# Where the load of S2 stands in the order of issue

## The chip, the cores and the metric

The kernel runs on one core of one Trainium2 chip. The metric is the device time of one execution in microseconds. The engines of the core run instruction queues of their own: TensorE (PE in the profile) multiplies matrices, its weight loads are shown as PEld; VectorE (DVE), ScalarE (ACT) and GpSimd (POOL) do elementwise work; SyncE (SP) issues DMAs. ScalarE can issue DMAs too. An engine's instructions run in the order in which they stand in its queue, and wait on semaphores that other engines or landed DMAs raise.

## The reference

An attention with a polynomial sketch as its feature map, followed by a Fourier mixing layer with an MLP. Cut to what matters here:

```python
# batch 4, heads 4, seq 1088, head_dim 32, r 8; S1, S2: [8, 32]
def phi(x):
    a = np.einsum('rd,bhsd->bhsr', S1, x)
    b = np.einsum('rd,bhsd->bhsr', S2, x)
    return np.einsum('bhsi,bhsj->bhsij', a, b).reshape(*x.shape[:-1], r * r)
q_p, k_p = phi(q), phi(k)
kv = np.einsum('bhsf,bhsd->bhfd', k_p, v)
z = np.sum(k_p, axis=2)
x = np.einsum('bhsf,bhfd->bhsd', q_p, kv) / (np.einsum('bhsf,bhf->bhs', q_p, z)[..., None] + 1e-06)
# x as [batch, seq, 128]
u = x + np.real(fft(fft(x, axis=1), axis=2))
out = u + np.maximum(normalised(u) @ w_ch1, 0) @ w_ch2
```

Everything in the attention goes through S1 and S2: both are needed, transposed, before the first feature of q or k can be computed.

## The kernel before

The program is a list of named steps, each with an engine. Nothing schedules them: a hand-written string, `ORDER`, gives the order of issue of all steps, and so the order within each engine's queue. A second table (`BANK`) gives each step its banks of PSUM, and `BEHIND` lets a SyncE load wait for an earlier one, counted back in SyncE's list of transfers.

The steps that matter for the change:

- `ld_s1` (SyncE) and `ld_s2` (ScalarE), both line 108, load S1 into rows 0 to 7 and S2 into rows 8 to 15 of one small tile, `s12`, in four copies side by side (4 KB each, in pieces of 128 bytes).
- `a_sin` (ScalarE, line 251) is an activation whose only purpose is to load ScalarE's first table.
- `warm` and `FILL` (TensorE, lines 90 and 92) are matmuls on zeros whose results nobody reads. Four stand at the start, others are put before a step: one in fp32 and two in bf16 before `s_t`, three in bf16 before `qf0.0` and `qf0.1`.
- `c_idb` (GpSimd) builds an identity, `c_id16` (ScalarE, line 308) casts its corner.
- `s_t` (TensorE, line 341) transposes `s12` with that corner. It waits for both loads and for `c_id16`.
- `s_use` (VectorE, lines 346 to 349) makes three tiles of the result: `sblk` for the projections of k, `sa` and `sb` for the features of q.
- `qT` (VectorE, line 430) and `kT` (line 381) transpose q and k; `qf` (TensorE, line 437) and `kpr` (line 363) project them; `qa` and `kab` (ScalarE, lines 444 and 415) copy one factor out of PSUM, `qp` (VectorE, line 448) and `kp` (GpSimd or VectorE, line 104) multiply the two factors.
- `vc` (ScalarE or GpSimd, line 97) rearranges v, `kv` (TensorE, line 397) and `pnd` (line 483) are the two products of the attention, and `den`, `rden`, `x` (lines 490, 495, 498) divide.

The four batches follow one another through these steps, overlapping; then come the Fourier rows (line 523) and the mixer by tiles of 512 rows. All loads but `ld_s2` are issued by SyncE: two halves of q of batch 0, S1, two halves of k of batch 0, two halves of q of batch 1, then v, the remainders of q and k (`qt`, `kt`), and the later batches. Buffers are double or triple, so loads of later batches wait for readers of the earlier ones.

Each DMA signals on one of eight semaphores, given out in rotation; a DMA that takes a semaphore again first waits until the previous DMA on it has landed. In the program of before, `ld_s2` stands on the same semaphore as `ld_s1`. It stands behind `a_sin` in ScalarE's queue.

Of the kernel before, what the change touches and what calls it, by code (L numbers as in the profile page):

```python
# [877 lines left out]
}  # L878

ORDER = """  # L880
c_wz warm ld_q0.0 c_iota c_rows ld_q0.1 ld_s1 c_bias c_eo1 a_sin ld_s2 c_xd0 ld_k0.1 c_vt0 c_more c_vt1 c_kk t_turn1
t_turn3 c_idb t_ph3 ld_k0.0 ld_q1.0 ld_q1.1 ld_v0.0 qT0.0 c_id16 s_t t_ph1 c_cen c_mask qT0.1 s_use ld_qt c_v10 kT0.1
ld_v0.3 ld_kt kT0.0 qf0.0 ld_k1 ld_v0.2 kpr0.1 ld_v0.1 ld_vt0 c_v11 ld_vt1 d_turn qa0.0 t_turn2 l_turn ld_v1.0 qT1.0
kpr0.0 ld_q2.1 t_ph2 kab0 qp0.0 qT1.1 qf0.1 c_kvz t_cos1 t_sin1 c_sgn kp0.3 ld_v1.3 kp0.1 qa0.1 ld_v1.2 qf1.0 qa1.0
# [51 lines left out]
```

## Time and profile before

| | |
|---|---|
| median of 3 runs | 89.14 us (89.13 to 90.52) |
| the profiled execution | 89.34 us |
| its span, first to last instruction | 87.3 us |
| mean granted TensorE clock | 0.961 |
| busy: TensorE matmuls, VectorE, ScalarE, GpSimd | 73.7, 63.8, 52.2, 49.6 us |
| DMA queue of SyncE | 15896 packets, 10.13 MB |
| DMA queue of ScalarE | 184 packets, 0.14 MB |

The span is that of the profile; what lies between it and the 89.34 us is start and end of the execution. Busy times of the engines overlap, and a high share only says that an engine works most of the time. What sets the time is read from the chain of work that ended last, which follows back from the last instruction, at each step, to what released it. The transfers are listed in it as DMA with the tile they fill; the tile `s12` appears as `t_s`.

### The profile page before, as it was taken

What the parts mean: (1) busy time and instruction counts of PE and PEld (TensorE: products, weight loads), DVE (VectorE), ACT (ScalarE), POOL (GpSimd) and SP (SyncE); (2) the same over time, 40 slices, a digit from 0 to 9 for tenths busy, and PEclk for the clock granted to TensorE, in tenths of its full rate; (3) what the DMA queues carried; (4) which work ended last, traced back from release to release, by engine and by line L of the source; (5) the groups of instructions that cost most, each with busy time, mean ns of one, the idle gap of its engine ahead of it and who ended that gap; (6) DMA issues with size and microseconds to landing.
All of it is one profiled execution on the core that took longest, in us unless ns stands there. A gap on an engine that the chain in (4) does not pass through costs nothing.

```text
span 87.3 us, 3321 instructions
## 1 busy us (share of the span) xinstructions
PE 73.7 (84%) x1380; PEld 53.4 (61%) x1380; DVE 63.8 (73%) x185; ACT 52.2 (60%) x94; POOL 49.6 (57%) x78
## 2 busy tenths in 40 slices
PE   5950399978997999989999779999999998898920
PEld 1300247436896868869794577797677575574920
DVE  5770292949999495799199985968796788877940
ACT  6020004763788855768718459274998698988620
POOL 7888300599739999879999970040599362100000
PEclk9999555899999999999999999999999999999999
DMA  0999599456984827910000020901202496423072
GB/s 15 266 265 261 106 249 234 76 151 187 304 265 135 275 62 220 245 30 0 8 8 8 0 60 0 66 2 21 46 0 60 135 67 181 156 105 138 25 261 103
DMA packets 16095, 10.47 MB, mean 120 GB/s; under 512 B 6864, under 2 KB 14544, under 8 KB 16080
## 3 DMA queue, kind: packets, MB, share of 16 engines
q1 hardware_dynamic: 15896, 10.13, 45.9%
q8 instruction: 10, 0.16, 0.9%
q10 hardware_dynamic: 184, 0.14, 0.5%
q14 instruction: 5, 0.04, 0.2%
HBM read 7.22 MB, written 2.23 MB: 108 GB/s over the span
## 4 chain that ended last, share of the span: by engine, by line
PE 46%; ACT 16%; DVE 14%; DMA 14%; issue 3%; POOL 1%; SPq 1%; DVEq 0%; ACTq 0%
DMA t_s<-in_S_dram 9%; PE ps L483 8%; PE ps L437 7%; PE ps L649 6%; PE ps L665 6%; PE ps L397 5%; DMA t_unT__166<-t_un__161 4%; PE ps L363 4%; ACT t_ht__168 L656 4%; PE ps L92 3%; DVE t_qp__124 L448 3%; DVE t_zr__139 L547 2%; ACT t_qa__123 L444 2%; PE ps L523 2%; PE ps L460 2%
## 5 line engine op out<-in xcount | busy, mean ns | idle before, releaser
L104 POOL TENSOR_TENSOR t_kp__118<-t_ab__116 128x512 f32<-128x512 f32 x7 | 7.3, 1068 | 7.7 <-ACT t_ab__116 L415 7.7
L444 ACT COPY t_qa__122<-ps 128x1024 f32<-128x1024 f32 x4 | 4.0, 1012 | 9.2 <-PE ps L437 9.2
L92 PE MATMUL ps<-t_wz 128*128 128x512 bf16 x18 | 7.5, 512 | 1.9 <-DVE t_wz L173 1.0
L104 POOL TENSOR_TENSOR t_kp__119<-t_ab__117 128x512 f32<-128x512 f32 x7 | 7.4, 1085 | 1.9 <-ACT t_ab__117 L415 1.9
L656 ACT ACTIVATE t_ht__168<-ps 128x1024 bf16<-128x1024 f32 x6 | 6.0, 1022 | 0.7 <-PE ps L649 0.7
L656 ACT ACTIVATE t_ht__167<-ps 128x1024 bf16<-128x1024 f32 x5 | 5.1, 1022 | 1.5 <-DVE t_st__147 L596 0.8
L483 PE MATMUL ps<-t_kvz,t_qp__124 128*64 128x66 f32 x128 | 4.3, 224 | 1.6 <-DVE t_qp__125 L448 1.1
L444 ACT COPY t_qa__123<-ps 128x1024 f32<-128x1024 f32 x4 | 4.0, 1012 | 2.6 <-PE ps L437 2.6
L483 PEld LDWEIGHTS ps<-t_kvz,t_qp__124 128*64 128x64 f32 x128 | 4.0, 137 | 1.9 <-DVE t_qp__125 L448 1.2
L649 PEld LDWEIGHTS <-t_w1b 128*128 128x128 bf16 x40 | 3.2, 97 | 3.0 <-issue 2.1
L448 DVE TENSOR_TENSOR t_qp__124<-ps,t_qa__122 128x1024 f32<-128x1024 f32 x2 | 2.4, 1224 | 3.3 <-ACT t_qa__122 L444 3.3
L397 PEld LDWEIGHTS ps<-t_v__121,t_kp__119 128*64 128x64 f32 x128 | 4.1, 138 | 0.7 <-issue 0.7
L92 PEld LDWEIGHTS <-t_wz 128*128 128x128 bf16 x18 | 1.7, 115 | 4.4 <-issue 3.1
L483 PEld LDWEIGHTS ps<-t_kvz,t_qp__125 128*64 128x64 f32 x128 | 3.9, 137 | 0.8 <-ACT t_kvz L97 0.4
L397 PE MATMUL ps<-t_v__121,t_kp__119 128*64 128x33 f32 x128 | 4.4, 224 | 0.0
L397 PE MATMUL ps<-t_v__120,t_kp__118 128*64 128x33 f32 x128 | 4.3, 223 | 0.0
L104 POOL TENSOR_TENSOR t_eo__133<-t_xd__132 128x516 bf16<-128x516 bf16 x4 | 4.1, 1050 | 0.2
L483 PE MATMUL ps<-t_kvz,t_qp__125 128*64 128x66 f32 x128 | 4.2, 223 | 0.0
L448 DVE TENSOR_TENSOR t_qp__124<-ps,t_qa__123 128x1024 f32<-128x1024 f32 x2 | 2.4, 1224 | 2.4 <-ACT t_qa__123 L444 2.4
L397 PEld LDWEIGHTS ps<-t_v__120,t_kp__118 128*64 128x64 f32 x128 | 4.1, 138 | 0.1
L341 PE MATMUL ps<-t_id,t_s 16*128 16x16 f32 x1 | 0.3, 253 | 4.6 <-DMA t_s<-in_S_dram 4.6
L97 ACT COPY t_kvz<-ps 64x66 f32<-64x66 f32 x8 | 1.7, 209 | 3.9 <-PE ps L397 3.4
(272 smaller groups left out, 233.2 us busy)
## 6 DMA issues: line engine op xcount, KB each, us to landing
t_q_in__109<-in_q_dram SPq DMA_DIRECT2D x4, 256.0 KB, 3.2
t_v_in__107<-in_v_dram SPq DMA_DIRECT2D x8, 128.0 KB, 4.2
t_k_in__106<-in_k_dram SPq DMA_DIRECT2D x2, 512.0 KB
t_v_in__108<-in_v_dram SPq DMA_DIRECT2D x8, 128.0 KB, 4.3
t_k_in__105<-in_k_dram SPq DMA_DIRECT2D x2, 256.0 KB
t_q_in__110<-in_q_dram SPq DMA_DIRECT2D x2, 256.0 KB
t_q_in__111<-in_q_dram SPq DMA_DIRECT2D x2, 256.0 KB
t_k_in__105<-in_k_dram SPq DMA_DIRECT2D x1, 512.0 KB
```

Source lines behind the costliest of these rows:

```text
L92: nc.tensor.matmul(T("ps")[:, free, :], w[:, 0:128], bass.AP(tensor=w.tensor, offset=w.offset, ap=[list(w.ap[0]), [0, 4], [1, 128]]), star ...
L104: return (nc.vector if engine == DVE else nc.gpsimd).tensor_tensor(out=out, in0=in0, in1=in1, op=op)
L363: nc.tensor.matmul(ps(use, 64 * t, [[1, 64]], 64 * c, 64), view(src, 128 * t + 64 * c, [[1, 64]]), T("sblk")[:], start=True, stop=True, ti ...
L397: nc.tensor.matmul(ps(f"kv{b}", 33 * pr, [[1, 33]], 64 * c, 64), kp, v, start=(t == 0), stop=(t == 8), tile_position=(0, 64 * c), skip_gro ...
L437: nc.tensor.matmul(ps(f"q{b}.{pr}", 512 * g + 256 * w, [[1, 256]], 64 * h, 64), view(T(src), 0, [[1, F]], 32 * g, 32), view(T(f"qT{b % 2}" ...
L444: nc.scalar.copy(T(f"qa{pr}")[:], ps(f"q{b}.{pr}", 0, [[512, 4], [1, 256]]))
L448: nc.vector.tensor_tensor(out=view(T(f"qp{b % 2}"), 1024 * pr, [[32, 4], [128, 8], [1, 32]]), in0=ps(f"q{b}.{pr}", 256, [[512, 4], [32, 8] ...
L460: nc.tensor.matmul(ps("qt", 512 * j + 256 * w + 128 * (h // 2), [[1, 128]], 64 * (h % 2), 64), view(T(src), 0, [[1, F]], 32 * j, 32), view ...
L483: nc.tensor.matmul(ps(f"nd{b}", 512 * (s // 3) + 132 * (s % 3) + 66 * pr, [[1, 66]], 64 * c, 64), w, view(T("kvz"), 132 * b + 66 * pr, [[1 ...
L649: nc.tensor.matmul(ps(use, 128 * n * i, [[1, 128 * n]]), T("w1b")[:, 128 * c:128 * c + 128], own("unT", g)[:, 0:128 * n], start=True, stop ...
L656: nc.scalar.activation(out=out, in_=in_, func=ACT.Relu)
L665: nc.tensor.matmul(ps(u, where, [[1, 128]]), view(own("ht", g), (128 if g % 5 == 4 else 512) * c + 128 * t, [[1, 128]]), T("w2b")[:, c, :] ...
```

## The change

One name moves in `ORDER`, from behind `a_sin` to the second place:

```diff
 ORDER = """
-c_wz warm ld_q0.0 c_iota c_rows ld_q0.1 ld_s1 c_bias c_eo1 a_sin ld_s2 c_xd0 ld_k0.1 c_vt0 c_more c_vt1 c_kk t_turn1
+c_wz ld_s2 warm ld_q0.0 c_iota c_rows ld_q0.1 ld_s1 c_bias c_eo1 a_sin c_xd0 ld_k0.1 c_vt0 c_more c_vt1 c_kk t_turn1
```

In the built program this has two effects. ScalarE's queue begins with the DMA instruction of `ld_s2`, then comes the table load, then `a_sin`; the queues of the other engines hold the same instructions in the same order. And since `ld_s2` is now the first DMA of the program, the rotation of the eight semaphores starts with it: `ld_s2` waits for nothing, and the loads of SyncE that follow stand one semaphore further. The waits that differ for this are those of the first eight or so loads that reuse a semaphore:

| load of SyncE | waits before for | waits after for |
|---|---|---|
| v, first part of batch 0 | S1 | S1 and S2 |
| q remainder, 4 parts | q half 0, q half 1, first k, second k | q half 0, q half 1, (nothing new), first k |
| v, last part of batch 0 | first q of batch 1 | second k |
| k remainder | second q of batch 1 | first q of batch 1 |
| k of batch 1 | v, first part of batch 0 | second q of batch 1 |

The arithmetic is the same.

## The prediction

> **What bounds the kernel now.** I read the page's slices first, then the chain of waits, then the timelines of ScalarE, TensorE and SyncE over the first microseconds.
>
> ```profile
> PE   5950399978997999989999779999999998898920
> PEclk9999555899999999999999999999999999999999
> DMA  0999599456984827910000020901202496423072
> ```
>
> Each digit is the busy share of 2.18 us. TensorE works in the first slices, has a hole in the fourth and fifth (about 6 to 10 us), and is then on a low clock for three slices; from there on it is nearly always busy. So the only large hole is at the start, and the chain of waits, in order of time, says what it waits for:
>
> ```profile
> 1.78 2.85 DMA t_s<-in_S_dram
> 4.63 0.02 issue
> 4.65 5.26 DMA t_s<-in_S_dram
> 9.91 0.14 issue
> 10.04 0.25 PE ps L341
> 10.30 1.39 PE ps L92 x3
> 11.69 1.94 PE ps L437 x32
> 13.63 1.91 PE ps L363 x32
> 15.53 0.88 PE ps L92 x3
> 16.42 1.13 PE ps L437 x32
> 17.55 0.02 issue
> ```
>
> Columns are start, length and what. The load of S1 lands at 4.63. The load of S2 is issued 0.02 us later and needs 5.26 us, and only then can the transpose of S1 and S2 (step s_t, L341) run, on which all projections (L437 of q, L363 of k) depend. Those then run at half clock: the same three fills take 1.39 us at 10.30 and 0.88 at 15.53, the same 32 matmuls of a q feature 1.94 us at 11.69 and 1.13 at 16.42.
>
> ```profile
> 0.71 1.28 ACT L251 ACT_TABLE_LOAD   x1 [0.71 <-PEq L920]
> 2.01 0.20 ACT L251 ACTIVATE t_scr<-t_hpi 128x1 f32<-128x1 f32 x1
> 4.65 0.58 ACTq L108 DMA_DIRECT2D t_s<-in_S_dram  x1
> 5.27 0.20 ACT L308 CAST t_id<-t_idb 16x16 f32<-16x16 bf16 x1 [3.06 <-POOL t_mask L101]
> ```
>
> ScalarE is free at 2.21 and issues S2 only at 4.65. In the program of before the load of S2 signals on the same one of the eight DMA semaphores as the load of S1, and so first waits for S1's landing. The table load and the activation cost it little; that wait costs it 2.44 us, and the position behind a full DMA queue the rest.
>
> **The change part by part.** S2's load becomes ScalarE's first instruction, at about 0.71. It becomes the first DMA, takes the first semaphore, and waits for nothing. No instruction is added or removed. The instructions of TensorE, VectorE, GpSimd and SyncE keep their order; the semaphores rotate by one, so some waits name another transfer.
>
> *ScalarE.* The issue takes 0.58 us (row at 4.65), so table load and activation end at about 2.8 instead of 2.21. The next ScalarE work, the identity's cast at 5.27, waited behind S2's issue; without it, it runs when GpSimd's identity is ready, before 5.27. Cost: nothing, under an idle stretch of 3.06 us.
>
> *SyncE.* Its loads are issued in the same order:
>
> ```profile
> 0.72 1.01 SPq L143 DMA_DIRECT2D t_q_in__109<-in_q_dram  x2
> 4.64 0.80 SPq L129 DMA_DIRECT2D t_v_in__107<-in_v_dram  x1
> 7.97 0.31 SPq L129 DMA_DIRECT2D t_v_in__107<-in_v_dram  x1
> 9.60 0.39 SPq L113 DMA_DIRECT2D t_kt_in<-in_k_dram  x1
> ```
>
> The load of v at 4.64, issued beside S2, took 0.80 us, a like one alone 0.31: two issues at once cost SyncE up to 0.49 us. Now q's first load, at 0.72, is the one beside S2, so every load behind it may slip by 0 to 0.49; I take 0.35. Against this, the rotation makes v at 7.97 wait for a load one earlier (k instead of q), the k remainder at 9.60 for the first q half of batch 1 instead of the second (which v at 7.97 waited for), and the 512 KB of k behind it for that second half. I put the two together at nothing for the loads after 10 us. The load of v at 4.64 now waits for S2 as well as S1; S2 is ahead of S1 by a microsecond at the issue, so that costs nothing unless S2 is starved (a rival below).
>
> *The transpose s_t.* Three things gate it. S1: 4.63, or 5.1 with the slip. S2: issued at 0.71; the two rows for a landing of this size are 2.85 (S1, nearly empty queues) and 5.26 us (S2, full ones), so 3.6 to 6.0; I take the shorter, since at 0.71 the queues are as empty as they were for S1. And TensorE's own queue, fills that run until 5.48:
>
> ```profile
> 1.04 1.89 PE L92 MATMUL ps<-t_wz 128*128 128x512 bf16 x4 [1.04 <-DVE t_wz L173]
> 4.42 1.06 PE L92 MATMUL ps<-t_wz 128*128 128x512 bf16 x2
> ```
>
> So s_t starts at 5.5 in place of 10.04: **4.54 us earlier** (4.0 if S2 takes 5.26 us). The fills are the cover for the slip of S1.
>
> The Trainium skill speaks against expecting more from the second issuer: "DMA: Bandwidth & Descriptors", section "Issuing engines are not separate DMA queues", says that transfers issued by different engines run on the same 16 DMA engines and interleave, and that only issue time is saved. By that alone S2 would share with the first q load, and the sum would be the same; the 0.80 and 0.58 us above show that here even the issue isn't free.
>
> *The clock.* Granted clock by stretch:
>
> ```profile
> core 0: us, PE busy (x) PEld busy (x) DVE busy (x) ACT busy (x) POOL busy (x), PEclk, DMA share, GB/s
> 0.00:5.50 5.50, 4.45 (x8) 1.39 (x8) 4.03 (x25) 1.72 (x4) 4.23 (x21) 1.00 0.56 163
> 5.50:8.90 3.40, 0.00 (x0) 0.00 (x0) 0.60 (x1) 0.28 (x1) 2.95 (x6) 1.00 1.07 262
> 8.90:15.70 6.80, 5.66 (x69) 3.25 (x70) 3.59 (x8) 1.13 (x2) 0.54 (x1) 0.50 0.92 196
> ```
>
> The full clock was granted from 5.5 to 8.9, where TensorE did nothing; after that idle stretch it fell to 0.50 until 15.7. With s_t at 5.5 there is no idle stretch, and I take it that the full clock stays. Three terms shrink to their full-clock twins: fills 1.39 to 0.88, q feature 1.94 to 1.13, k projection 1.91 to 1.15 (row below). Together **2.08 us**. The row's 1.00 before 5.5 isn't borne out by the durations: 1.89/4 = 0.47 us per fill is the half-clock value (1.39/3 = 0.46).
>
> The Trainium skill, "TensorE: Matmul & The Clock Gate", Part 1, says that half rate is the default, and that a free-running window of about 3.4 us decides, so its phase may differ between runs. The trace agrees on an idle stretch of that length (5.5 to 8.9) followed by 0.50; what another phase would do is the first rival.
>
> What VectorE does in between must keep up. Its last q transpose ends at 6.10, the three ops on S gave way to the next after 0.40 us (10.41 to 10.81), and the two k transposes took 1.29:
>
> ```profile
> 5.40 0.70 DVE L430 STREAM_TRANSPOSE t_qT__114<-t_q_in__109 128x512 f32<-128x512 f32 x1
> 10.41 0.22 DVE L346 TENSOR_TENSOR t_sblk<-ps,t_mask 128x64 f32<-128x64 f32 x1 [4.31 <-PE ps L341]
> 10.81 1.29 DVE L381 STREAM_TRANSPOSE t_kT__112<-t_k_in__105 128x512 f32<-128x512 f32 x2
> 23.07 1.15 PE L363 MATMUL ps<-t_sblk,t_kT__113 128*64 128x64 f32 x32
> ```
>
> So S is ready at about 6.5, just before the fills end (5.5 + 0.25 for s_t + 0.88 = 6.63), the q feature runs to 7.8, and the k transposes end at 7.9 if k has landed, just in time. The second q feature then ends at 17.55 - 4.54 - 2.08 = 10.93: 6.62 us earlier.
>
> *What is late next: the loads.* They do not start earlier, and the compute behind them comes 6.6 us sooner. The tightest ones:
>
> ```profile
> t_q_in__109<-in_q_dram SPq DMA_DIRECT2D x4, 256.0 KB, 3.2
> 19.93 0.43 SPq L143 DMA_DIRECT2D t_q_in__111<-in_q_dram  x1
> 27.81 0.69 DVE L430 STREAM_TRANSPOSE t_qT__114<-t_q_in__111 128x512 f32<-128x512 f32 x1
> 29.66 0.38 DVE L495 RECIPROCAL t_den__126<-t_den__126 128x36 f32<-128x36 f32 x1 [1.16 <-ACT t_den__126 L490]
> SPq L129 <- DMA t_k_in__105<-in_k_dram: 1.5, 1, 1.5
> 29.24 0.31 SPq L129 DMA_DIRECT2D t_v_in__107<-in_v_dram  x1
> 32.63 1.20 DVE L381 STREAM_TRANSPOSE t_kT__112<-t_k_in__105 128x1024 f32<-128x1024 f32 x1
> 34.85 1.22 DVE L448 TENSOR_TENSOR t_qp__124<-ps,t_qa__123 128x1024 f32<-128x1024 f32 x1 [1.01 <-ACT t_qa__123 L444]
> ```
>
> The second q half of batch 2, issued at 19.93, lands by the median of 3.2 us at 23.1. Its transpose would be wanted at 27.81 - 6.62 = 21.2: 1.9 us late, of which the 1.16 us that VectorE idles before the reciprocal absorbs most, so 0.75 is given back. The k of batch 2 lands at 29.24 (the v load waits for it) and would be wanted at 26.0: 3.2 late, of which 1.01 is idle before the next product: 2.2 given back. That landing may itself move, since SyncE's later waits on compute go away. I take the middle, **1.4 us given back**. Beyond 38 us no inputs are loaded, and the shift carries through to the end.
>
> Sum: 4.54 + 2.08 - 1.4 = 5.2 us. The profiled execution took 89.34 us (span 87.3 and 2.0 around it), which gives 84.1; the median is 0.2 below the profiled run: **83.9**. Its own range, from no give-back (6.6) to all of 2.2 (4.4): 82.5 to 84.8.
>
> **The rivals.** *Half clock at first* (0.13): the release comes only after 12.3, at the second boundary. The terms at half clock stay, the fills at 15.53 become half-clock ones (+0.51), and the shift is 4.54 - 0.51 = 4.0: 85.1. For it: TensorE's durations before 5.5 are half-clock ones. Against it: the row for 5.5 to 8.9 grants 1.00.
>
> *The loads decide all* (0.13): no idle time absorbs, and what can be won is the slack of k of batch 2, 32.63 - 29.24 = 3.4 us: 85.7. For it: the DMA slices are 9s from 2 to 9 us and again from 11 to 15. Against it: the idle times in the rows above.
>
> *No effect* (0.07): S2, in 128-byte pieces, still lands near 10 us, because its queue gets little service beside SyncE's until the DMA slices drop; the load chain's slip stays inside its slack: 89.
>
> *Slower* (0.07): the same late S2, but now the load of v at 4.64 waits for it, since it has S2's semaphore, and all loads behind it on SyncE with it. With S2 at 9.9 they slip by 5.3 us; k of batch 2 lands at 34.5, 1.9 us after its transpose began: 91.0. It decides from a slip of 3.4 us, that is from S2 landing after 8.0. For it: 5.26 us for 4 KB in before. Against both: S1, of the same size and behind 512 KB of q in its queue, took 2.85.
>
> **How the numbers follow.** The forecast has 0.60, with 83.9. The range must reach the first two rivals: 82.3 to 86.0 holds nearly all of the forecast, half clock and most of the load case, about 0.82. A difference of 2% is 1.8 us, about what the runs of before can tell from none (89.13 to 90.52). Faster: 0.60 + 0.13 + 0.13 = 0.86; within: 0.07; slower: 0.07.
>
> **What would show it.** S2's issue as ScalarE's first row; s_t directly behind the fills, at 5.5; no slice with an empty TensorE before 10 us and no 5s in its clock; the second q feature ending near 11; and new waits of VectorE or ScalarE on loads of q, v or k between 18 and 30 us, which the chain of waits should name. I am wrong if s_t still waits for a DMA beyond 6 us, if the v load of 4.64 is issued much later, or if the clock falls in spite of a busy TensorE.

## The result and the profile after

| | before | after |
|---|---|---|
| median | 89.21 us (89.13 to 90.52, 4 runs) | 82.78 us (82.31 to 84.42, 4 runs) |
| profiled execution, its span | 89.34, 87.3 us | 82.31, 80.2 us |

The ratio is 0.9264, with a 95% interval of 0.9202 to 0.9326: 6.4 us between the medians. The forecast was 83.9. Measured twice more on other chips, the same kernel gave 0.9394 (0.9265 to 0.9522; 83.98 against 88.51 us) and 0.9435 (0.9335 to 0.9535; 84.02 against 88.55 us). The medians of the three sets differ by 6.4, 4.5 and 4.5 us where 5.2 were forecast, so the gain is sure and its size is known to about a microsecond either way. What follows compares mainly kernels of one set, which share the runs of the kernel before. Some executions of every kernel run some per cent longer than the rest; the ratios leave these out on both sides, the medians do not.

The page's slices of the profile after, each 2.0 us:

```profile
PE   4999995998899998999995999989999979899910
PEclk9999999999999999999999999999999999999999
DMA  0989979648597970982002120020032955314082
```

The hole of TensorE between 6 and 10 us is gone, and with it the 5s in its clock. The timeline of the first microseconds (start, length, engine, line, what):

```profile
0.71 0.60 ACTq L108 DMA_DIRECT2D t_s<-in_S_dram  x1
0.72 1.01 SPq L143 DMA_DIRECT2D t_q_in__109<-in_q_dram  x2
...
4.70 0.68 SPq L129 DMA_DIRECT2D t_v_in__107<-in_v_dram  x1
5.42 0.28 PE L341 MATMUL ps<-t_id,t_s 16*128 16x16 f32 x1
5.63 1.29 PE L92 MATMUL ps<-t_wz 128*128 128x512 bf16 x3
...
6.86 0.69 PE L437 MATMUL ps<-t_qT__114,t_sa 32*64 32x256 f32 x16
...
7.91 1.15 PE L363 MATMUL ps<-t_sblk,t_kT__112 128*64 128x64 f32 x32
...
8.99 0.82 PE L92 MATMUL ps<-t_wz 128*128 128x512 bf16 x3
...
9.74 0.69 PE L437 MATMUL ps<-t_qT__114,t_sa 32*64 32x256 f32 x16
...
10.22 0.64 PE L437 MATMUL ps<-t_qT__114,t_sb 32*64 32x256 f32 x16
```

S2 is the first issue, the transpose s_t follows at 5.42, and the second q feature ends at 10.22 + 0.64 = 10.86. In before its last row is 16.83 + 0.64 = 17.47 (the 17.55 of the chain of waits counts up to the step behind it), so it ends 6.61 us earlier. The first load of v, which now waits for S1 and S2, is issued at 4.70, so both have landed by then. The granted clock, busy times in the same stretch that was empty before:

```profile
5.50:8.90 3.40, 3.40 (x68) 1.96 (x68) 2.78 (x7) 0.82 (x1) 2.95 (x6) 1.00 1.10 260
8.90:15.70 6.80, 5.93 (x132) 3.59 (x136) 6.44 (x10) 4.18 (x7) 6.29 (x8) 1.00 0.81 187
```

The chain of waits no longer passes through S2 but through the loads behind it, up to the Fourier rows of batch 0 (L523):

```profile
1.77 2.85 DMA t_s<-in_S_dram
...
6.39 4.73 DMA t_qt_in<-in_q_dram
...
11.19 4.63 DMA t_v_in__107<-in_v_dram
...
15.83 4.64 DMA t_q_in__111<-in_q_dram
...
21.59 5.49 DMA t_k_in__105<-in_k_dram
27.07 0.02 issue
27.10 1.25 DVE t_kT__112 L381
...
31.34 1.95 PE ps L523 x30
```

From 6 to 27 us it is one load after another, the second and third issued when an earlier one has landed; between the third and the fourth stand 1.1 us of VectorE. From L523 to the end nothing changed: in before that step began at 38.52 with 48.8 us of span left, here at 31.34 with 48.9.

### The profile page after: what moved, and what is told of

Same layout as the page of the kernel before. It is cut to its first block, busy times and chain, and to the rows that moved or that the text cites. A ratio compares the mean times of both kernels' runs of the same rounds, so it can differ in the third digit from the quotient of the medians.

```text
span 80.2 us, 3321 instructions
## 1 busy us (share of the span) xinstructions
PE 71.0 (88%) x1380; PEld 52.1 (65%) x1380; DVE 63.7 (79%) x185; ACT 52.3 (65%) x94; POOL 49.7 (62%) x78
## 4 chain that ended last, share of the span: by engine, by line
DMA 33%; PE 29%; DVE 18%; ACT 10%; SPq 3%; issue 2%; DVEq 0%; ACTq 0%
PE ps L649 7%; PE ps L665 7%; DMA t_k_in__105<-in_k_dram 7%; DMA t_qt_in<-in_q_dram 6%; DMA t_q_in__111<-in_q_dram 6%; DMA t_v_in__107<-in_v_dram 6%; PE ps L483 6%; DMA t_unT__166<-t_un__161 5%; ACT t_ht__168 L656 4%; DMA t_s<-in_S_dram 4%; DVE t_qp__124 L448 3%; PE ps L397 3%; DVE t_zr__139 L547 3%; PE ps L523 2%; DVE t_x__129 L498 2%; DVE t_x__131 L498 2%
## 5 line engine op out<-in xcount | busy, mean ns | idle before, releaser
L104 POOL TENSOR_TENSOR t_ph<-t_xd__132 128x516 bf16<-128x516 bf16 x1 | 1.1, 1051 | 5.2 <-DVE t_ph L104 5.2
L104 POOL TENSOR_TENSOR t_xd__132<-t_x__131 128x567 bf16<-128x567 bf16 x1 | 1.3, 1262 | 4.1 <-DVE t_xd__132 L104 4.1
L448 DVE TENSOR_TENSOR t_qp__124<-ps,t_qa__122 128x1024 f32<-128x1024 f32 x2 | 2.4, 1220 | 1.5 <-ACT t_qa__122 L444 1.5
```

Of the source, the lines that this page charges most:

```text
L104: return (nc.vector if engine == DVE else nc.gpsimd).tensor_tensor(out=out, in0=in0, in1=in1, op=op)
L448: nc.vector.tensor_tensor(out=view(T(f"qp{b % 2}"), 1024 * pr, [[32, 4], [128, 8], [1, 32]]), in0=ps(f"q{b}.{pr}", 256, [[512, 4], [32, 8] ...
```

## The experiments

In the diffs a minus line is the changed kernel's, unless said. The start of L523 in the chain of waits serves as the mark at which a kernel has left its input stage.

**The clock alone.** The edit is made to the kernel of before.

```diff
-    "s_t": (1, 2, 0), ...
+    "s_t": (1, 18, 0), ...
```

> The kernel of before with S2 still loaded late, and 16 more bf16 fills ahead of the transpose, so that TensorE is busy from 1 to about 9.5 us. Theory (the clock is a part of the gain of its own): s_t stays at about 10.0 us, the granted clock stays at 1.00, fills, q feature and k projection take 0.88, 1.13 and 1.15 us in place of 1.39, 1.94 and 1.91, and the time falls by 2.1 us, to about 87.1. Rival (only the earlier S2 counts, the clock's part is swallowed by later waits): 88.7 to 89.2.

Median 86.95 us (85.49 to 89.78) against 89.93 (87.64 to 91.67) for the kernel before; there is no interval for this pair. Counted as the ratios are, this kernel has two executions, 85.49 and 85.60, and the kernel before four, 87.64 to 88.64: 2.6 us between the means, where 2.1 were expected. The chain of waits:

```profile
10.23 0.75 PE ps L92 x3
10.99 1.05 PE ps L437 x32
12.04 1.08 PE ps L363 x32
13.12 0.75 PE ps L92 x3
13.87 1.13 PE ps L437 x32
```

S2 is as late as ever, and fills, q feature and k projection take 0.75, 1.05 and 1.08 us where before they took 1.39, 1.94 and 1.91: 2.36 us less for the three, and the second q feature ends at 15.0 in place of 17.55. The clock is a part of its own, and matmuls that compute nothing buy it. The profiled execution also lacks a stall that the trace of before has, of about 0.8 us in the first q feature of batch 2 (it comes up again below), so not all of a difference between these two traces is the clock's.

**The wait or the place.** S2 is put behind the table load and its activation, but ahead of SyncE's loads in the rotation of semaphores.

```diff
-c_wz ld_s2 warm ld_q0.0 c_iota c_rows ld_q0.1 ld_s1 c_bias c_eo1 a_sin c_xd0
+c_wz c_bias a_sin ld_s2 warm ld_q0.0 c_iota c_rows ld_q0.1 ld_s1 c_eo1 c_xd0
```

> S2 stays on ScalarE and behind the table load and its activation, but is taken ahead of the SyncE loads in the rotation of semaphores, so that it waits for no other load. Theory (the wait for S1's landing held S2 up, not the table): S2 is issued at about 2.3 us, lands 2.9 to 5.3 us later, s_t starts between 5.5 and 7.6, and the time is 82.8 to 84.9. Rival (the place ahead of the table is what brings it): S2 meets full queues as in before, lands near 9 us, and the time is 87 or more.

82.08 us (81.47 to 83.16), ratio 0.9247 (0.9148 to 0.9346). The timeline of ScalarE:

```profile
0.71 1.28 ACT L251 ACT_TABLE_LOAD   x1 [0.71 <-PEq L920]
1.04 0.57 ACTq L108 DMA_DIRECT2D t_s<-in_S_dram  x1
2.01 0.20 ACT L251 ACTIVATE t_scr<-t_hpi 128x1 f32<-128x1 f32 x1
```

S2 left even earlier than either theory had it, at 1.04 us, while the table was still loading and ahead of the activation that stands before it in the queue: here the issue of the DMA did not wait for the engine's work ahead of it, so what stands ahead of the prediction, that an engine's instructions run in the order of its queue, does not hold for it. The edit also moves `c_bias`, the constants that VectorE writes for this activation; they end at 1.00 here and at 1.65 in before. So the place in before could have cost S2 until about 1.7 us (an estimate from these rows), and what kept it until 4.65 was the wait for S1's semaphore. Run again beside the changed kernel:

> The changed kernel, as the measure for the three beside it: 82.3 to 84.0 us.

> S2 behind the table load in ScalarE's queue but waiting for no load, once more, beside the changed kernel. Theory (the wait for S1's landing was all of it, the place in ScalarE's queue is worth nothing): within 0.6 us of the changed kernel. Rival (the first place is worth something): 1 us or more slower.

0.9374 (0.9280 to 0.9467) against 0.9435 (0.9335 to 0.9535) for the changed kernel: no difference that these intervals tell. The place was worth nothing that shows; what counts is the rotation of the semaphores.

**Which engine issues.**

```diff
-    add("ld_s2", ACTE, "", "s12/1", lambda: ld_s(nc.scalar, 1, "S2"))
+    add("ld_s2", SP, "", "s12/1", lambda: ld_s(nc.sync, 1, "S2"))
-c_wz ld_s2 warm ... ld_s1 c_bias ...
+c_wz warm ... ld_s1 ld_s2 c_bias ...
```

> S2 issued by SyncE right behind S1, on its own semaphore. Theory (S2 only has to be early and wait for nothing; which engine issues it doesn't matter): it lands 0.2 to 0.5 us after S1, at about 5.0, s_t starts at 5.4 to 5.5, all loads behind it slip by the 0.45 us of one issue, and the time is that of the changed kernel plus 0 to 0.5. Rival (ScalarE's own queue matters): s_t later than 6 us, and the time 84 or more.

The changed kernel was run once more in the same set:

> The changed kernel once more, beside the others of this set. It should take 82.3 to 83.0 us. The stall of TensorE's own sequencer in the first q feature of batch 2 (0.8 us in the trace of before, 0.7 and 0.9 in the kernels without first fills and with a late transpose, none in the changed kernel): if it belongs to the program, there is none here; if it comes and goes with the execution, it may appear, and the time is then up to 0.9 us longer.

S2 by SyncE: 83.62 us, ratio 0.9431 (0.9345 to 0.9518), s_t at 5.4. The changed kernel: 83.98 us (82.79 to 85.93), 0.9394 (0.9265 to 0.9522), its median above the expected range. Its trace, like the first one of this kernel, has no stall in the first q feature of batch 2 (32 matmuls from 25.58 to 26.71), which would suit a stall that belongs to the program; but the first q feature of batch 3 runs from 30.75 to 32.28 there, 1.53 us, where it took 1.12 in the first trace. S2 has to be early and wait for nothing; who issues it doesn't matter within these intervals.

**Without the first fills, and with a late transpose.**

```diff
-WARM = 4
+WARM = 0
-    "s_t": (1, 2, 0), "qf0.0": (0, 3, 0), ...
+    "qf0.0": (0, 3, 0), ...
```

> The changed kernel without the matmuls on zeros ahead of the transpose. Theory (they gate s_t at 5.4 us, but buy the clock): s_t starts at about 4.9 us, when the identity is cast, and the projections run at half clock at first: q feature 1.94 and k projection 1.91 us, the second q feature ends 1 to 2 us later than in the changed kernel (10.9), and the time is 83.5 to 84.8. Rival (the fills only hold s_t up): 82.3, half a microsecond faster.

```diff
-    "s_t": (1, 2, 0), ...
+    "s_t": (1, 9, 0), ...
```

> The changed kernel with seven more bf16 fills ahead of the transpose: s_t moves from 5.4 to about 7.5 us with TensorE busy and the clock up, the three fills behind it then take 0.88 in place of 1.29 us, so the second q feature ends about 1.6 us later. Theory (compute sets the time, the loads give back little): the whole 1.6 us shows at the end, about 84.4. Rival (the loads set the time once S2 is early): at most 0.5 us shows, 82.8 to 83.3.

Without fills: 84.38 us, 0.9423 (0.9376 to 0.9471). Late transpose: 84.25 us, 0.9427 (0.9380 to 0.9475). TensorE's timeline, first three rows without fills, last two with the late transpose:

```profile
4.93 0.28 PE L341 MATMUL ps<-t_id,t_s 16*128 16x16 f32 x1 [4.93 <-ACT t_id L308]
5.14 1.46 PE L92 MATMUL ps<-t_wz 128*128 128x512 bf16 x3
10.57 0.64 PE L437 MATMUL ps<-t_qT__114,t_sb 32*64 32x256 f32 x16
```

```profile
7.19 0.23 PE L341 MATMUL ps<-t_id,t_s 16*128 16x16 f32 x1
11.47 0.64 PE L437 MATMUL ps<-t_qT__114,t_sb 32*64 32x256 f32 x16
```

The fills do hold s_t up, by 0.5 us, and give it back in clock: without them the second q feature ends at 11.21, 0.35 later than in the changed kernel and not the 1 to 2 expected, since the half clock lasted only into the first q feature (its halves take 1.16 and 0.88 us, in the changed kernel 0.69 and 0.64). In this set, in which the changed kernel was not run, the variant with S2 behind the table ended that step at 10.42 (9.78 + 0.64), this one at 11.21, the late transpose at 12.11, and the ratios are 0.9247, 0.9423 and 0.9427; the first interval lies below the two others. The step from 10.42 to 11.21 cost 1.8%, the next 0.9 us nothing that shows. That isn't a straight line, and the traces show what else differs. The variant ended that step early not by s_t (5.37) but because its three fills took 0.82 us, where the other executions with the same fills ahead of s_t have 0.86 to 1.39; so the end of the half clock at the start differs from execution to execution. And in both later kernels TensorE stalls in the first q feature of batch 2, in the variant it doesn't. The chain of waits without fills:

```profile
25.50 1.00 PE ps L437 x18
26.50 0.72 issue
27.21 0.74 PE ps L437 x14
```

These 32 matmuls take 2.46 us, with the late transpose 2.60 and in the variant 1.13. Run again later, the variant had a ratio of 0.9374. So these ratios don't price a late s_t.

**The loads, freed.** Four of SyncE's loads no longer wait for earlier ones of the list (the expectation says five); the second kernel has the S2 of the variant above as well.

```diff
-    "ld_v0.0": 5, "ld_v0.1": 6, "ld_vt0": 6, "ld_q2.1": 6, "ld_v1.3": 3, "ld_q2.0": 6, "ld_q3.1": 5, ...
+    "ld_v0.0": 5, "ld_vt0": 6, "ld_q3.1": 5, ...
```

> The changed kernel without five of the waits of SyncE's loads for earlier ones (second, third and fourth v of batch 0 and 1, both halves of q of batch 2). The q half for which VectorE waits 1.3 us is issued about 0.8 us earlier, when the k of batch 1 has landed. Theory of the prediction (late loads cost time at the end): 0.3 to 0.8 us faster than the changed kernel. Rival (VectorE's waits for loads are swallowed by idle time behind them): within 0.2 us of it.

> The same free loads together with S2 behind the table load but waiting for nothing (the earlier variant, in which S2's issue overlapped the table load). If the loads limit, this is the fastest kernel so far, 81.3 to 82.0; if not, 82.0 to 82.6 like that variant.

83.12 us, 0.9313 (0.9172 to 0.9455), and 83.26 us, 0.9372 (0.9271 to 0.9472), against 0.9394 (0.9265 to 0.9522) for the changed kernel in the same set: inconclusive as times, since the first ratio is where the theory had it but the intervals overlap over most of their width. The chain of waits of the first:

```profile
25.83 0.60 PE ps L437 x10
26.43 0.11 issue
26.54 1.11 PE ps L437 x22
```

The chain now runs through compute there, and TensorE stalls in the first q feature of batch 2: from 25.83 to 27.65 where an undisturbed one takes 1.13. The profile shows nothing that it waits for. In before the same step had the same gap (32 matmuls from 31.83 to 33.72), in the changed kernel it had none. The second kernel has the same gap (25.90 to 27.64). In both L523 starts at 32.45, no earlier than the 32.28 of the changed kernel in this set.

**One issue less on SyncE.**

```diff
-    add("ld_s1", SP, "", "s12/0", lambda: ld_s(nc.sync, 0, "S1"))
+    add("ld_s1", ACTE, "", "s12/0", lambda: ld_s(nc.scalar, 0, "S1"))
-c_wz ld_s2 warm ... ld_q0.1 ld_s1 c_bias ...
+c_wz ld_s2 ld_s1 warm ... ld_q0.1 c_bias ...
```

> Both S2 and S1 issued first by ScalarE, so SyncE has one issue (0.45 us) less ahead of all its loads but the first two. s_t stays at 5.4 us, behind the fills. Theory of the prediction (from 18 to 30 us late loads cost time at the end): loads of q and k land 0.3 to 0.5 us earlier and the time falls by as much, to 0.3 to 0.5 below the changed kernel. Rival (relieved of the loads, TensorE's own sequencer stalls instead, as in the two kernels with free loads): within 0.2 us.

83.25 us (82.76 to 84.68), 0.9442 (0.9354 to 0.9530), beside 0.9435 for the changed kernel: no gain. Its chain of waits:

```profile
29.61 0.35 PE ps L437
29.96 1.29 issue
31.25 1.12 PE ps L437 x31
32.37 1.89 PE ps L523 x27
```

The loads are off the chain, and TensorE's own stall is on it, one q feature further on and 1.29 us long. That is what the rival expected.

**The loads, held up.**

```diff
-    "ld_v0.0": 5, ...
+    "ld_v0.0": 1, ...
```

> The changed kernel with the first v load waiting for the landing of the second q half of batch 1 (about 9.6 us) in place of S1 and S2, so that it and all loads behind it on SyncE slip; by the issues in between, the k of batch 1 leaves at about 13 in place of 10. This is the price of the rival in which S2's semaphore holds the loads up, with s_t still at 5.4. Theory (loads and compute are about level after the change): nearly all of the 2.5 to 3 us shows, 84.8 to 86. Rival (loads have room): less than 1 us, below 84.

89.55 us (89.17 to 91.74), ratio 1.0153 (1.0061 to 1.0246): slower than the kernel before by some 1.5%, and 5.5 us above the changed kernel's median where the theory had 2.5 to 3, with s_t still at 5.4. Waits, chain and stretches of clock:

```profile
DVE t_qtT L454 <- DMA t_qt_in<-in_q_dram: 2.4, 1, 2.4
```

```profile
10.45 2.77 DMA t_qt_in<-in_q_dram
...
22.14 3.81 PE ps L397 x72
...
26.52 3.95 PE ps L483 x72
```

```profile
8.90:15.70 6.80, 3.79 (x74) 1.63 (x74) 4.41 (x8) 3.68 (x5) 5.59 (x8) 1.00 0.59 161
15.70:24.00 8.30, 8.30 (x144) 7.41 (x144) 6.69 (x13) 4.06 (x6) 3.13 (x5) 0.54 0.73 173
```

The q remainder arrives late, VectorE stands 2.4 us, TensorE goes without work for some 3 us (busy 3.79 of 6.80), and then the clock falls: 0.54 from 15.7 to 24 and 0.62 from 24 to 32, so that the attention products take 3.81 and 3.95 us where they took 2.22 and 2.33. So of the 5.5 us some 2.4 are VectorE's wait and some 3.2 these two products at the low clock (an estimate from these rows).

## Why the prediction was right, step by step

**S2 and s_t: right.** 5.42 for the forecast 5.5, gated by the fills, as said.

**The cost at SyncE: wrong, and harmless.** I charged the loads up to 0.49 us for an issue beside ScalarE's. SyncE's first two issues take 1.01 us in both traces, with S2 beside them and without. The load of v at 4.70, now alone, still takes 0.68 us, so the 0.80 of before needn't have come from S2's issue.

**The clock: right in mechanism and sum, not in its terms.** The fall from 8.9 to 15.7 is gone. From the start of s_t to the end of the second q feature 1.99 us are saved, and 2.08 were forecast. But the first three fills give only 0.16 us of it (1.23 from start to start in place of 1.39), not 0.51: they take 1.29 us, the next three 0.82, although the row from 5.5 to 8.9 grants 1.00. q feature and k projection give 0.89 and 0.83, not 0.81 and 0.76, and the second three fills 0.13, which I had at nothing: the 0.88 that I took for their full-clock length was in part half clock, which the row of before has until 15.7. That these errors cancel, and that the second q feature ends 6.61 us earlier where 6.62 were forecast, is luck in part. The kernel with only the fills added confirms that the clock is worth 2 us and more.

**The give-back by late loads: the term that was mis-sized.** I took 1.4 us from a bound of 0 to 2.2. In the profiled execution there was less than none: L523 began 38.52 - 31.34 = 7.18 us earlier, 0.57 more than the second q feature. Two things stood behind it. First, in before TensorE stalled for about 0.8 us in the first q feature of batch 2 (1.89 us where it takes 1.13), which I hadn't priced; without that stall some 7.4 us would have been due (an estimate, 6.61 + 0.76), so the loads took back about 0.2. Second, VectorE did wait for loads, but less than I had it:

```profile
20.50 0.71 DVE L430 STREAM_TRANSPOSE t_qT__114<-t_q_in__111 128x512 f32<-128x512 f32 x1 [1.26 <-DMA t_q_in__111<-in_q_dram]
...
27.10 1.25 DVE L381 STREAM_TRANSPOSE t_kT__112<-t_k_in__105 128x1024 f32<-128x1024 f32 x1 [0.63 <-DMA t_k_in__105<-in_k_dram]
```

The wait for q of batch 2 fell on its first half, not on the second as I had it, and the idle time behind took up most of it. k of batch 2 landed at 27.07 and not at 29.24: by my own reckoning 1.0 us late (27.07 against 32.63 - 6.61), not 3.2, and the idle time behind it in before (1.01 and 0.47 us, part of it the stall's doing) took up most of that. That landing is not steady: its stretch in the chain, 5.49 us here, is 6.48 and 6.99 in the two later traces of the same kernel, and there L523 began at

```profile
28.04 1.25 DVE t_kT__112 L381
...
32.28 1.95 PE ps L523 x30
```

```profile
28.33 1.25 DVE t_kT__112 L381
...
32.57 1.95 PE ps L523 x30
```

which is 1.1 and 1.4 us of give-back by the same reckoning; in the first of the two 0.4 of it are TensorE's, in the 1.53 us of the q feature just ahead. So the step named the right transfer, and 1.4 is about what it costs in some executions and 0.2 in the one that the result shows. The medians of these two sets, 83.98 and 84.02, lie at the forecast of 83.9, though with the kernel before 0.7 us faster there; that of the result lies 1.1 below it.

**The rivals.** *Half clock at first* did not happen beyond the first three fills. *No effect* and *Slower* did not happen, since S2 had landed by 4.70. *The loads decide all* is half true: after the change they are on the chain of waits, but freeing them gained nothing that the intervals tell, and in those traces TensorE's own stall stands in their place. The price of *Slower*, 91.0, was no great exaggeration: holding the same loads up gave 89.55 even with s_t early.

**Open.** What TensorE's sequencer waits for in the q features of batches 2 and 3 was not found. The stall is there or not, and sits in different places, in kernels that differ little. The traces' records of DMA transfers show one regularity: in each of the six with a long stall (before, no first fills, late transpose, both kernels with freed loads, both loads on ScalarE) it ends 1.3 to 1.8 us after a transfer of 16 KB on the queue that the page calls q8 instruction has ended. In before that transfer runs from 30.14 to 31.10 and the stall ends at 32.62; in the changed kernel's first trace it runs from 21.41 to 22.49, well ahead of that q feature at 25.31. That TensorE waits there for its own instructions would fit, but no run moves these transfers, so it is not shown.

## What to carry to other kernels

Look at what a DMA's issue waits for before moving it: here two loads that have nothing to do with each other shared a completion semaphore by the order in which they were handed out, and one name moved in a list took the wait away. A wait that left TensorE idle for some 3 to 5 us was paid twice here, once as idle time and once as half clock behind it, in a gain as in a loss. When a wait at the start goes, expect the next bounds close behind: here the loads and TensorE's own stall are both within a microsecond or two of compute, and relieving the loads alone showed nothing.

## What the hardware showed that was not expected

ScalarE issued a DMA at 1.04 us in the middle of a table load that ran from 0.71 to 1.99. The granted clock is given as 1.00 for the first 5.5 us in every trace, but the fills there, where a kernel has them, take 0.47 us each (four in 1.89), the length that they have in the stretch at 0.50; so a 1.00 in these first rows is no sign that matmuls run at full speed there. The issue of a 128 KB load of v by SyncE took from 0.31 to 2.47 us in the trace of before. And 2.4 us of waiting for a load led to a mean clock of 0.54 over the 8.3 us from 15.7 to 24.
